# Softmax attention and a 2-D spectral filter in one kernel: the later weight pads on GpSimd, one small product on ScalarE, and a new planned order

## The chip, the cores and the metric

The kernel runs on one core of a Trainium2 chip. A core has five engines, each with its own instruction queue that runs in order: TensorE (PE, matmuls; PEld in the profile is its weight load), VectorE (DVE), ScalarE (ACT), GpSimd (POOL) and SyncE (SP, which here issues most of the DMAs). The metric is the device time of one execution in microseconds; lower is better. Times of the kernel before are those of three runs, and the profile is of one more execution.

## The reference

One input `x` of 2048 rows and 448 columns goes through two branches, which a gate mixes row by row:

```python
g = sigmoid((x * gate_w).sum(-1, keepdims=True))
a = softmax_attention(x, wqkv) @ wo        # 16 heads of 28 columns, no mask
b = irfft2(rfft2(x) * (w_r + 1j * w_i))    # over both axes, S=2048, D=448
return g * a + (1 - g) * b
```

Attention has 16 heads x 2048 x 2048 scores. All tensors are bfloat16.

## The kernel before

**Attention.** The heads are taken in four groups of four. A head's 28 columns are padded to 32, so that four heads fill the 128 partitions: `Wp` holds the padded query and key weights. Group 0's weights are padded early on POOL (`pq0`, `pk0`), those of groups 1 to 3 later on DVE (`pq1`, `pk1`, line 479), as copies from the raw weights (`raw`, which the profile shows as `Z`, whose space it uses) to `Wp`. They wait for the loads `wq1` and `wk1`, which a small POOL write each releases on SP. Queries are projected in chunks of 512 (`qT`), keys into `kT`, values into `V`.

The scores are made in tiles of 128 keys x 512 queries for one head: 1024 tiles, in 16 chunks of 64. A tile is exponentiated in one of two ways. ACT reads one or two neighbouring PSUM banks and writes `exp` into `PA` (line 1276; early tiles go into `oT`, whose space is free then). Or DVE writes an integer form of the exponent into `PD` (line 1300), and POOL adds two constants to groups of up to three such tiles (line 1108, two instructions a group); the three integer tiles, read as bfloat16, are each multiplied by `V`, and their sum approximates the exponential. So an ACT tile costs PE one score and one value matmul, and a DVE tile one score and three value matmuls. Value matmuls add up in a PSUM bank for a chunk, which is then normalised (`normalise`) and later multiplied by `Wo`.

Matmuls are narrow. A score uses 30 rows of TensorE's array, and four heads can run side by side ("row" mode); a value matmul uses 32 columns, and four can run side by side ("col" mode). `mc` splits a wide matmul into such strips.

**Squares and the largest key.** Keys and queries carry a column with half their squared length. For it a projected chunk is squared, either by ACT (`e_pj_sq`, line 696) or by DVE in two instructions (`e_pj_sd`, lines 702 and 704). The parameter `qdn` says how many of the 16 query chunks, counted from the last, use DVE: 15 here. For groups 1 to 3 a chain `largest` (`kw1` to `kw3`) finds the longest key: POOL squares the keys (`e_ks`, line 737), a matmul adds them up, DVE takes a maximum (`e_kx_m1`, line 745), DVE multiplies a 128 x 4 constant by it (`e_kx_sp`, line 748, tile `m1`), a matmul transposes that, DVE takes a maximum again (line 754), a matmul spreads it and DVE copies it (line 760). The queries of the group need the result.

**The filter.** POOL folds `x` (`e_xf`, lines 845 and 847: `xr` and in place `xt`, four passes of each), then come matmuls with constant tables in stages F1 to F6, with DVE evictions between (lines 856, 893, 906, 923, 936 to 938).

**Order.** Nothing is scheduled while it runs. A planner in the kernel's own Python places every task in time by simple costs per engine (ACT 0.051 us + columns/1200, DVE 0.065 us + columns/960) and a latency between engines, and the program is the list of tasks in that order; each engine then runs its own part in order, with semaphores. Units (a projection, a filter stage) have a target time, `target + OFF[name]`, and the dictionary `PAR` has the limits by which score tiles are shared out: `dve_lead` and `pool_lead` (how far DVE's and POOL's planned work may run ahead when DVE takes a tile), `n_dve` (the most tiles for DVE), `hold`, `slack` and `cp` (when DVE stops taking tiles of a chunk), `k3`, `w3`, `w2` (which run of banks ACT is given), `a21`. With `a21` over 0 a third score tile joins a pair as a single ACT tile only if ACT's planned backlog is at most `a21` microseconds; with 0 this test is left out:

```python
            if PAR["a21"] > 0 and P.backlog("ACT") > s + PAR["a21"]:
                return None
```

POOL tasks that are ready are taken by key, lowest first; `xr` and `xe` of block k have the keys 0.5 k and 0.5 k + 0.1 (about -5 for k = 0).

Of the kernel before, what the change touches and what calls it, by code (L numbers as in the profile page):

```python
# [12 lines left out]
ACT = mybir.ActivationFunctionType  # L13
ALU = mybir.AluOpType
# [151 lines left out]
def cols(n):  # L166

    return max(n / 2400.0 + 0.003 + 0.000016 * n, 0.026)


def dve(n):

    return 0.065 + n / 960.0


def act(n):
    return 0.051 + n / 1200.0
# [124 lines left out]

class Kernel:

    PAR = dict(T=368, margin=0, dve_lead=1.065, pool_lead=10.679, early=374.528, dmargin=0.3, join=0.1, veff=0.9, vnext=4, vnb=3, nfa=2, nfd=2, flush=0.2, hold=4, n_dve=380.349, late=8, fill=1, cp=1.617, slack=0.884, zgap=0.6, vurg=24.799, nfa2=5, nfd2=0, trk=0.361, vrk=2.7, fitm=0.02, ukeep=3, dkeep=0, k3=2, w3=0.3, w2=0.091, amax=2, ulate=16.42, dsolo=0, k21=0, a21=1, qdn=15)


    OFF = dict(X0=5.19, X1=-27.98, X3=0.84, X5=5.45, X6=-20.0, q0_0=-17.13, k0_0=0.4, k0_0b=14.3, k0_1=31.05, k0_2=-0.87, k0_3=24.59, v0_0=-34.41,
               v0_1=5.02, v0_2=34.02, v0_3=39.07, q0_1=-26.85, q0_2=-9.67, q0_3=-1.37, gate=-42.87, F1_0=21.01, F1_1=-0.1, F1_2=-18.79, F1_3=10.64,
               F1_4=6.41, F1_5=-3.3, F1_6=13.27, F1_7=-3.83, F1_8=-19.35, F1_9=-37.58, F1_10=-31.96, F1_11=-3.0, F1_12=8.24, F1_13=12.19, F1_14=10.6,  # L310
               F1_15=3.05, k1_0=-6.72, k1_1=11.73, k1_2=-10.54, k1_3=2.77, kw1=-2.6, v1_0=59.93, v1_1=-7.41, v1_2=33.97, v1_3=16.69, q1_1=3.56,
               q1_2=31.48, q1_3=43.95, F2_0=-56.04, F3_0=39.53, F5_0=34.29, F2_1=-37.91, F3_1=-1.85, F5_1=20.99, F2_2=-0.01, F3_2=13.06, F5_2=15.59,
               F2_3=-0.41, F3_3=24.43, F5_3=21.39, F2_4=-20.67, F3_4=-0.44, F5_4=-15.95, F2_5=-51.59, F3_5=20.45, F5_5=30.74, F2_6=-22.67,
               F3_6=-11.91, F5_6=0.76, F2_7=15.58, F3_7=-27.34, F5_7=40.78, F2_8=-45.05, F3_8=-2.08, F5_8=1.99, F2_9=1.89, F3_9=-4.53, F5_9=5.02,
               F2_10=-20.81, F3_10=-2.03, F5_10=-2.65, F2_11=-61.46, F3_11=-48.73, F5_11=6.72, F2_12=-31.48, F3_12=4.76, F5_12=-2.58, F2_13=8.64,
               F3_13=-22.22, F5_13=-47.39, F2_14=37.5, F3_14=29.27, F5_14=1.07, F2_15=-29.45, F3_15=10.64, F5_15=1.27, k2_0=-1.49, k2_1=-12.56,
               k2_2=-0.3, k2_3=-2.61, kw2=18.08, q2_0=17.63, v2_0=18.18, v2_1=0.51, v2_2=50.32, v2_3=17.26, q2_1=3.35, k3_0=4.85, k3_1=-26.48,
               k3_2=17.52, k3_3=-22.9, kw3=-30.88, q3_0=13.8, v3_0=-18.7, v3_1=-4.44, v3_2=21.94, v3_3=-1.69, q3_1=0.48, q2_2=-0.95, q3_2=1.88,
               q2_3=0.3, rg0=-13.79, rg1=-54.48, rg2=-36.06, rg3=-18.67, F6_0=-50.79, F6_1=5.4, F6_2=-3.55, F6_3=-15.05, F6_4=-36.03, F6_5=-0.33,
               F6_6=-35.14, F6_7=-32.01, F6_8=-28.36, F6_9=-21.44, F6_10=-29.11, F6_11=-16.4, F6_12=-3.59, F6_13=-18.37, F6_14=-0.2, F6_15=-2.28,  # L320
               o_0=25.95, o_1=8.69, o_2=-0.63, o_3=3.15, o_4=48.45, o_5=31.19, o_6=-15.24, o_7=27.38, o_8=18.41, o_9=5.1, o_10=-1.7, o_11=13.87,
               o_12=29.43, o_13=5.28, o_14=16.72, o_15=-1.66)


    NB = 8
# [96 lines left out]
    def head(self):  # L422
# [3 lines left out]
        dep = self.dep = {}  # L426
# [31 lines left out]
        gate = {}  # L458
# [16 lines left out]
        def pad(name, eng, qk, g0, g1, deps, dur, key=-8):  # L475
            src = self.raw[:, :, 448 * qk + 112 * g0:448 * qk + 112 * g1].rearrange("p c (h d) -> p c h d", d=28)
            o = self.Wp[0:112, :, qk, 4 * g0:4 * g1, 0:28]
            e = {"DVE": nc.vector, "POOL": nc.gpsimd}[eng]
            dep[name] = P.add(eng, dur, lambda: e.tensor_copy(out=o, in_=src), deps=deps + [m], key=key)
# [4 lines left out]
        for s in range(4):  # L484
            dep[f"wo{s}"] = P.add("SP", 0.42, lambda s=s: self.dma(self.Wo[32 * s:32 * s + 28, :, :], wo4[s]),
                                  deps=[dep["woz"]], land=8.0, key=50)
        pad("pq1", "DVE", 0, 1, 4, [dep["wq1"]], 0.75, -0.4)
        pad("pk1", "DVE", 1, 1, 4, [dep["wk1"]], 0.75, -0.4)

        for r, src in enumerate((self.w_r, self.w_i)):  # L490
            s3 = src.rearrange("(a b) f -> a b f", b=128)
# [19 lines left out]
    def make_units(self):  # L511
        U = self.U = {}
        dep = self.dep
        T = self.T = self.PAR["T"]

        def unit(name, target, phases, deps=(), **k):
            u = U[name] = Unit(name, target + self.OFF.get(name, 0.0), phases, deps, **k)
            self.P.units.append(u)
            return u
# [12 lines left out]
        def proj(qk, g, c, target):  # L532
# [14 lines left out]
            sq = [("ACT", act(512), self.e_pj_sq, (qk, g, c))]  # L547
            if qk == 0 and n >= 16 - self.PAR["qdn"]:
                sq = [("DVE", dve(512), self.e_pj_sd, (qk, g, c, 0)), ("DVE", dve(512), self.e_pj_sd, (qk, g, c, 1))]
# [37 lines left out]
        def largest(g, t0):  # L587

            unit(f"kw{g}", t0, [("PE", cols(512), self.e_kx_pe, (g,), "col"), ("DVE", 0.62, self.e_kx_m1, (g,)),
                                ("DVE", 0.1, self.e_kx_sp, (g,)), ("PE", 0.03, self.e_kx_tr, (g,), "col"), ("DVE", 0.25, self.e_kx_mm, (g,)),  # L590
                                ("PE", 0.04, self.e_kx_bc, (g,), "col"), ("DVE", 0.12, self.e_kx_kc, (g,))],
                 [dep[f"ks{g}_{c}"] for c in range(4)] + [dep["cA2"], dep["mxz"]], rank=-1)
        nc = self.nc
# [19 lines left out]
        for c in range(4):  # L613
            proj(1, 1, c, (0.10 + 0.025 * c) * T)
        largest(1, 0.18 * T)
        proj(0, 1, 0, 0.20 * T)
        values(1, 0.21 * T, 0.01 * T)
# [5 lines left out]
        for c in range(4):  # L623
            proj(1, 2, c, (0.30 + 0.03 * c) * T)
        largest(2, 0.40 * T)
        proj(0, 2, 0, 0.42 * T)
        values(2, 0.43 * T, 0.015 * T)
        proj(0, 2, 1, 0.5 * T)
        for c in range(4):
            proj(1, 3, c, (0.515 + 0.015 * c) * T)  # L630
        largest(3, 0.565 * T)
        proj(0, 3, 0, 0.575 * T)
        values(3, 0.58 * T, 0.01 * T)
# [111 lines left out]
        self.nc.vector.tensor_reduce(out=self.mc1[:], in_=b, axis=AX.X, op=ALU.max)  # L745

    def e_kx_sp(self, b, g):
        self.nc.vector.tensor_scalar(out=self.m1[:], in0=self.cA[:, 685:689], scalar1=self.mc1[:, 0:1], scalar2=None, op0=ALU.mult)  # L748

    def e_kx_tr(self, b, g):  # L750
        self.mm(b[0:4, 0:4], self.cA[:, 681:685], self.m1[:], pos=(0, 0))
# [253 lines left out]
    def stream(self):  # L1005
        P, nc, U, PAR = self.P, self.nc, self.U, self.PAR
        packs = [[(n, g, c, i, h) for i in range(16) for h in range(4)] for n, (g, c) in enumerate(self.chunks)]
# [65 lines left out]
        def take_dve(busy, k):  # L1073
            out = []
            for n in range(st["chunk"], 16):
                L = [p for p in packs[n] if p not in busy]
                if n == 15:
                    L = L[:max(0, len(L) - int(PAR["hold"]) - 4)]
                elif len(packs[n]) <= PAR["hold"]:
                    continue  # L1080
                elif max(P.backlog("POOL"), P.free["PE"]) + PAR["cp"] > P.free["PE"] + 0.36 * len(packs[n]) + PAR["slack"]:
                    continue
# [573 lines left out]
```

## Time and profile before

| | |
|---|---|
| time, median of 3 runs | 375.91 us (375.65 to 376.28) |
| the profiled execution | 376.95 us, its span 375.2 us |
| mean granted TensorE clock | 0.986 |
| PE busy | 363.3 us, 97% of the span |
| ACT busy | 355.2 us, 95% |
| DVE busy | 327.9 us, 87% |
| POOL busy | 319.6 us, 85% |

The profiled execution took 1.04 us more than the median of the runs. Lines of the profile read: engine or line, operation, output tile <- input tile with its shape, count, then busy microseconds, mean nanoseconds of one, idle time just before them and what ended it. In a timeline row the first number is the start and the second the time, both in microseconds, and what stands in brackets is the idle time of that engine ahead of it, with its releaser; neighbouring instructions of a kind are merged (x3). In a row of waits stand the waiting engine and line, what it waited for, and then the total, the number of times and the longest.

### The profile page before, as it was taken

How to read it: one execution, taken by the hardware profiler on the slowest of the kernel's cores; microseconds unless marked ns; L12 is line 12 of the kernel's file. 1: busy time of each engine (PE TensorE's matmuls, PEld its weight loads, DVE VectorE, ACT ScalarE, POOL GpSimd, SP SyncE). 2: the span in 40 equal slices, each digit the busy share in tenths (PEclk: the TensorE clock that was granted, in tenths of full speed). 3: DMA queues.
4: the chain of work that ended last, by engine and by line, in shares of the span. 5: the costliest groups of instructions: out<-in, count | busy, mean ns of one | idle time of the engine just before them, and what ended most of it. 6: DMA issues, size and time to landing. Idle time of an engine off the chain costs nothing.

```text
span 375.2 us, 15055 instructions
## 1 busy us (share of the span) xinstructions
PE 363.3 (97%) x6526; PEld 140.4 (37%) x6526; DVE 327.9 (87%) x564; ACT 355.2 (95%) x411; POOL 319.6 (85%) x262
## 2 busy tenths in 40 slices
PE   8979999999999999999999999999999999999995
PEld 5434332334334334344343433333333333233332
DVE  5696899989996999999999789899999899998962
ACT  3977999999999999999999999999999999999993
POOL 7953789997899989988799998869988899899991
PEclk9977999999999999999999999999999999999999
DMA  8654400000000012112111021100000000001001
GB/s 263 137 105 66 129 27 3 2 3 3 28 3 18 28 28 59 42 42 79 48 45 28 17 57 30 37 21 3 3 2 14 28 14 14 2 17 38 26 15 51
DMA packets 18968, 14.77 MB, mean 39 GB/s; under 512 B 7923, under 2 KB 18517, under 8 KB 18902
## 3 DMA queue, kind: packets, MB, share of 16 engines
q1 hardware_dynamic: 17542, 13.01, 13.0%
q8 instruction: 51, 0.84, 1.0%
q10 hardware_dynamic: 1360, 0.81, 0.8%
q14 instruction: 15, 0.12, 0.1%
HBM read 11.97 MB, written 3.68 MB: 42 GB/s over the span
## 4 chain that ended last, share of the span: by engine, by line
PE 59%; ACT 22%; DVE 12%; issue 4%; DMA 1%; POOL 1%; DVEq 0%; SPq 0%; ACTq 0%
PE bank L400 58%; ACT PA L1276 22%; DVE PD L1300 5%; PE bank L678 1%; DMA Z<-in_A_wqkv_dram 1%; DVE AB L936 1%; DVE xt L938 1%; DVE sq L704 1%; DVE xt L937 1%; DVE sq L702 1%; DVE m L748 1%; DVE kT L717 0%; DVE mc L745 0%; DVE oraw L969 0%; POOL xr L845 0%
## 5 line engine op out<-in xcount | busy, mean ns | idle before, releaser
L1276 ACT ACTIVATE PA<-bank 128x1024 bf16<-128x1024 f32 (+1 forms) x386 | 340.4, 1088 | 7.1 <-PE bank L400 6.6
L1108 POOL TENSOR_SCALAR PD<-PD 128x1536 int16<-128x1536 int16 (+2 forms) x190 | 269.0, 1417 | 40.5 <-DVE PD L1300 24.5
L1300 DVE TENSOR_SCALAR PD<-bank 128x512 int16<-128x512 f32 x273 | 180.1, 682 | 16.7 <-PE bank L400 14.6
L400 PE MATMUL bank<-qT,kT 30*128 30x512 bf16 x1024 | 143.8, 387 | 2.6 <-DVE kT L717 2.1
L400 PE MATMUL bank<-PD,V 128*32 128x512 bf16 x819 | 120.4, 383 | 0.0
L400 PE MATMUL bank<-PA,V 128*32 128x512 bf16 x735 | 118.1, 383 | 0.0
L400 PEld LDWEIGHTS <-kT 30*128 30x128 bf16 (+1 forms) x1040 | 38.4, 91 | 121.1 <-issue 114.2
L400 PEld LDWEIGHTS <-V 128*32 128x32 bf16 x1570 | 32.6, 94 | 43.3 <-issue 39.6
L400 PE MATMUL bank<-xT,Wp 112*32 112x512 bf16 (+3 forms) x528 | 40.8, 388 | 0.5 <-DVE PD L1300 0.2
L400 PE MATMUL bank<-Wv,xT 112*32 112x112 bf16 (+1 forms) x1024 | 19.9, 225 | 0.1
L400 PE MATMUL bank<-Wo,oT 128*32 128x448 bf16 x256 | 18.6, 356 | 0.3 <-DVE oT L988 0.3
L400 PEld LDWEIGHTS <-xT 112*32 112x32 bf16 x1024 | 15.3, 102 | 6.6 <-issue 6.1
L906 DVE TENSOR_TENSOR TT<-bank,Wf 128x900 bf16<-128x900 f32 x16 | 17.3, 1085 | 0.5 <-PE bank L400 0.5
L400 PEld LDWEIGHTS <-Wp 112*32 112x32 bf16 (+1 forms) x528 | 10.5, 96 | 15.4 <-issue 12.1
L737 POOL TENSOR_TENSOR oT<-kT 128x512 bf16<-128x512 bf16 x12 | 12.4, 1040 | 0.5
L923 DVE CAST Z<-bank 113x512 bf16<-113x512 f32 x16 | 10.8, 684 | 1.9 <-PE bank L400 1.7
L913 POOL TENSOR_TENSOR TT<-TT 128x225 bf16<-128x225 bf16 x16 | 9.0, 562 | 3.4 <-DVE TT L906 2.8
L988 DVE TENSOR_TENSOR oT<-bank,oraw 128x512 bf16<-128x512 f32 (+1 forms) x19 | 11.1, 599 | 0.7 <-PE bank L400 0.6
L717 DVE CAST kT<-bank 128x512 bf16<-128x512 f32 x15 | 10.1, 677 | 1.6 <-PE bank L400 1.6
L856 DVE CAST U__76<-bank 113x512 bf16<-113x512 f32 x16 | 10.6, 680 | 0.5 <-PE bank L400 0.5
L704 DVE TENSOR_TENSOR sq<-bank,sq 128x512 bf16<-128x512 f32 x15 | 10.4, 690 | 0.5
L702 DVE CAST sq<-bank 128x512 bf16<-128x512 f32 x15 | 10.2, 681 | 0.5 <-PE bank L400 0.5
(91 smaller groups left out, 283.9 us busy)
## 6 DMA issues: line engine op xcount, KB each, us to landing
cM<-cM SPq DMA_DIRECT2D x16, 128.0 KB, 2.2
cG<-cG SPq DMA_DIRECT2D x16, 128.0 KB, 2.1
Wf<-Wd SPq DMA_DIRECT2D x32, 56.2 KB, 2.3
out_dram<-fin SPq DMA_DIRECT2D x15, 112.0 KB, 1.7
xt<-in_A_x_dram SPq DMA_DIRECT2D x2, 448.0 KB
Z<-in_A_wqkv_dram SPq DMA_DIRECT2D x2, 294.0 KB
Wd<-in_B_w_r_dram SPq DMA_DIRECT2D x4, 112.5 KB, 6.2
Wd<-in_B_w_i_dram SPq DMA_DIRECT2D x4, 112.5 KB, 9.1
```

Source lines behind the costliest of these rows:

```text
L400: self.nc.tensor.matmul(out, lhsT=lhsT, rhs=rhs, start=start, stop=stop, skip_group_check=True, **k)
L702: self.nc.vector.tensor_copy(out=t, in_=b)
L704: self.nc.vector.tensor_tensor(out=t, in0=b, in1=t, op=ALU.mult)
L717: self.nc.vector.tensor_copy(out=self.kT[g % 2][:, 512 * c:512 * c + 512], in_=b)
L737: self.nc.gpsimd.tensor_tensor(out=self.oT[:, 3, 512 * c:512 * c + 512], in0=k, in1=k, op=ALU.mult)
L856: self.nc.vector.tensor_copy(out=o, in_=b[0:113, :].rearrange("p (c g e) -> p c g e", c=4, g=16))
L906: self.nc.vector.tensor_tensor(out=self.TT[bg % 2][:].rearrange("p w r f -> p w (r f)").rearrange("p w (r f) -> p w r f", r=2), in0=bc_at( ...
L923: self.nc.vector.tensor_copy(out=self.Z[:, :, :, :, 8 * bg:8 * bg + 8].rearrange("p c t s e -> p c (t s) e"), in_=b[0:113, :].rearrange("p ...
L988: nc.vector.tensor_tensor(out=self.oT[:, g, 512 * c + c0:512 * c + c1], in0=b[:, c0:c1], in1=oraw[:, c0:c1], op=ALU.mult)
L1108: nc.gpsimd.tensor_scalar(out=t[:, j, 0:n, :], in0=t[:, 0, 0:n, :], scalar1=float(sh), scalar2=1.0, op0=ALU.add, op1=ALU.mult)
L1276: nc.scalar.activation(out=buf, in_=src, func=ACT.Exp, scale=LN2 / 128.0)
L1300: nc.vector.tensor_scalar(out=dst, in0=self.bank[b], scalar1=C2, scalar2=0.0, op0=ALU.add, op1=ALU.max)
```

## The change

Three edits are in the code, and the planner's numbers are replaced. The pads of the later query and key weights go from DVE to POOL, with a planned 1.4 us instead of 0.75 and a key of -2 instead of -0.4. The small product in `largest` goes from DVE to ACT, with a planned 0.2 us instead of 0.1. All of `PAR` but `T` and a few others, and all of `OFF`, have new values; they were chosen outside the kernel, by an objective with a penalty on plans that use little of TensorE's array. That objective is not part of the code.

```diff
-    PAR = dict(T=368, margin=0, dve_lead=1.065, pool_lead=10.679, early=374.528, dmargin=0.3, join=0.1, veff=0.9, vnext=4, vnb=3, nfa=2, nfd=2, flush=0.2, hold=4, n_dve=380.349, late=8, fill=1, cp=1.617, slack=0.884, zgap=0.6, vurg=24.799, nfa2=5, nfd2=0, trk=0.361, vrk=2.7, fitm=0.02, ukeep=3, dkeep=0, k3=2, w3=0.3, w2=0.091, amax=2, ulate=16.42, dsolo=0, k21=0, a21=1, qdn=15)
+    PAR = dict(T=368, margin=0, dve_lead=1.156, pool_lead=14, early=807.331, dmargin=0.3, join=0.6, veff=0.95, vnext=2.765, vnb=2, nfa=6.029, nfd=2.924, flush=0.8, hold=2, n_dve=290, late=8, fill=1, cp=2.032, slack=2, zgap=0.25, vurg=25, nfa2=5, nfd2=0, trk=0.441, vrk=2.574, fitm=0.019, ukeep=3, dkeep=0, k3=3, w3=0, w2=0.2, amax=2, ulate=12, dsolo=0, k21=0, a21=0, qdn=8)
-    OFF = dict(X0=5.19, X1=-27.98, X3=0.84, X5=5.45, X6=-20.0, q0_0=-17.13, k0_0=0.4, k0_0b=14.3, k0_1=31.05, k0_2=-0.87, k0_3=24.59, v0_0=-34.41,
+    OFF = dict(X0=-0.45, X1=-29.9, X2=-10.5, X3=-11.1, X4=-4.99, X5=-7.62, X6=-28.51, X7=-25.13, k0_0=-4.85, k0_0b=10.57, k0_1=22.47, k0_2=-20.78,
...
-        pad("pq1", "DVE", 0, 1, 4, [dep["wq1"]], 0.75, -0.4)
-        pad("pk1", "DVE", 1, 1, 4, [dep["wk1"]], 0.75, -0.4)
+        pad("pq1", "POOL", 0, 1, 4, [dep["wq1"]], 1.4, -2)
+        pad("pk1", "POOL", 1, 1, 4, [dep["wk1"]], 1.4, -2)
...
-                                ("DVE", 0.1, self.e_kx_sp, (g,)), ("PE", 0.03, self.e_kx_tr, (g,), "col"), ("DVE", 0.25, self.e_kx_mm, (g,)),
+                                ("ACT", 0.2, self.e_kx_sp, (g,)), ("PE", 0.03, self.e_kx_tr, (g,), "col"), ("DVE", 0.25, self.e_kx_mm, (g,)),
...
     def e_kx_sp(self, b, g):
-        self.nc.vector.tensor_scalar(out=self.m1[:], in0=self.cA[:, 685:689], scalar1=self.mc1[:, 0:1], scalar2=None, op0=ALU.mult)
+        self.nc.scalar.activation(out=self.m1[:], in_=self.cA[:, 685:689], func=ACT.Copy, scale=self.mc1[:, 0:1])
```

More of the change, by code (lines that the diff above doesn't have):

```diff
@@ L303 @@
 class Kernel:
-    PAR = dict(T=368, margin=0, dve_lead=1.065, pool_lead=10.679, early=374.528, dmargin=0.3, join=0.1, veff=0.9, vnext=4, vnb=3, nfa=2, nfd=2, flush=0.2, hold=4, n_dve=380.349, late=8, fill=1, cp=1.617, slack=0.884, zgap=0.6, vurg=24.799, nfa2=5, nfd2=0, trk=0.361, vrk=2.7, fitm=0.02, ukeep=3, dkeep=0, k3=2, w3=0.3, w2=0.091, amax=2, ulate=16.42, dsolo=0, k21=0, a21=1, qdn=15)
-    OFF = dict(X0=5.19, X1=-27.98, X3=0.84, X5=5.45, X6=-20.0, q0_0=-17.13, k0_0=0.4, k0_0b=14.3, k0_1=31.05, k0_2=-0.87, k0_3=24.59, v0_0=-34.41,
[L309 to L322, printed above, removed]
@@ new lines @@
+    PAR = dict(T=368, margin=0, dve_lead=1.156, pool_lead=14, early=807.331, dmargin=0.3, join=0.6, veff=0.95, vnext=2.765, vnb=2, nfa=6.029, nfd=2.924, flush=0.8, hold=2, n_dve=290, late=8, fill=1, cp=2.032, slack=2, zgap=0.25, vurg=25, nfa2=5, nfd2=0, trk=0.441, vrk=2.574, fitm=0.019, ukeep=3, dkeep=0, k3=3, w3=0, w2=0.2, amax=2, ulate=12, dsolo=0, k21=0, a21=0, qdn=8)
+    OFF = dict(X0=-0.45, X1=-29.9, X2=-10.5, X3=-11.1, X4=-4.99, X5=-7.62, X6=-28.51, X7=-25.13, k0_0=-4.85, k0_0b=10.57, k0_1=22.47, k0_2=-20.78,
+               k0_3=32.55, kw0=10.25, v0_0=-12.45, v0_1=-29.57, v0_2=6.17, v0_3=32.53, q0_1=4.21, q0_2=-6.73, gate=15.58, F1_0=36.12, F1_1=0.69,
+               F1_2=-1.75, F1_3=17.53, F1_4=-13.39, F1_5=13.41, F1_6=16.94, F1_7=9.72, F1_8=0.25, F1_9=-25.08, F1_10=-51.88, F1_11=0.2, F1_12=5.78,
+               F1_13=26.43, F1_14=-2.48, F1_15=-2.49, k1_0=-8.16, k1_1=17.54, k1_2=2.77, k1_3=8.36, kw1=13.88, q1_0=-1.45, v1_0=52.1, v1_1=-1.06,
+               v1_2=39.22, v1_3=12.53, q1_1=10.96, q1_2=34.23, q1_3=45.93, F2_0=-52.96, F3_0=34.06, F5_0=-3.69, F2_1=-40.46, F5_1=18.45, F2_2=-4.76,
+               F3_2=-5.56, F5_2=38.59, F2_3=-5.36, F3_3=12.45, F5_3=0.43, F2_4=5.71, F3_4=-3.25, F5_4=-14.08, F2_5=13.74, F3_5=16.41, F5_5=-11.6,
+               F2_6=-1.94, F3_6=7.43, F5_6=-13.26, F2_7=13.57, F3_7=-6.19, F2_8=-55.51, F3_8=37.14, F5_8=-21.59, F2_9=-45.03, F3_9=-20.95,
+               F2_10=-1.55, F3_10=-32.87, F5_10=-26.13, F2_11=-48.8, F3_11=-43.35, F5_11=9.26, F2_12=-38.78, F3_12=1.02, F5_12=-0.32, F2_13=23.39,
+               F3_13=7.44, F5_13=-20.63, F2_14=14.62, F3_14=53.26, F5_14=-2.45, F2_15=-3.06, F3_15=16.65, F5_15=0.78, k2_0=-13.88, k2_1=6.57,
+               k2_2=-10.56, k2_3=-95.43, kw2=15.14, q2_0=33.8, v2_0=3.08, v2_1=-1.03, v2_2=28.31, v2_3=-2.27, q2_1=20.53, k3_0=-3.14, k3_1=-38.98,
+               k3_2=-15.49, k3_3=-42.81, kw3=1.34, q3_0=7.3, v3_0=-17.34, v3_1=-5.49, v3_2=42.42, v3_3=12.22, q3_1=-16.25, q3_2=-13.01, q2_3=-0.81,
+               q3_3=17.97, rg0=-5.85, rg1=-56.51, rg2=-35.51, rg3=-19.61, F6_0=-32.88, F6_1=-4.28, F6_2=0.57, F6_3=-2.16, F6_4=-1.15, F6_5=-49.81,
+               F6_7=-2.74, F6_8=25.8, F6_9=-11.59, F6_10=-16.07, F6_11=-39.7, F6_12=18.45, F6_13=-30.87, F6_14=17.71, F6_15=-0.8, o_0=38.37,
+               o_1=10.8, o_2=8.04, o_3=34.48, o_4=51.74, o_5=6.44, o_6=25.61, o_7=-2.77, o_8=-27.63, o_9=-2.51, o_10=-2.02, o_11=7.52, o_14=8.79,
+               o_15=-10.28)
```

## The prediction

> **What bounds the kernel now.** I read the page's engine shares first, then the busy time by stretch, then the waits of the two poor stretches, then the order of instructions where those waits end.
>
> ```profile
> PE 363.3 (97%) x6526; PEld 140.4 (37%) x6526; DVE 327.9 (87%) x564; ACT 355.2 (95%) x411; POOL 319.6 (85%) x262
> L1276 ACT ACTIVATE PA<-bank 128x1024 bf16<-128x1024 f32 (+1 forms) x386 | 340.4, 1088 | 7.1 <-PE bank L400 6.6
> 10.50:19.00 8.50, 7.97 (x125) 3.66 (x125) 5.01 (x7) 8.46 (x13) 8.34 (x5) 1.00 0.53 122
> 19.00:24.00 5.00, 2.43 (x32) 1.22 (x31) 4.93 (x9) 3.07 (x5) 3.93 (x3) 0.94 0.59 119
> 24.00:34.00 10.00, 10.00 (x231) 5.31 (x232) 6.66 (x15) 6.96 (x10) 3.81 (x4) 0.52 0.59 95
> 46.00:365.00 319.00, 315.54 (x5666) 117.19 (x5664) 293.16 (x504) 317.14 (x360) 285.30 (x224) 1.00 0.09 25
> 370.00:375.20 5.20, 1.07 (x20) 0.41 (x16) 2.04 (x6) 1.16 (x2) 0.00 (x0) 0.98 0.27 91
> ```
>
> The stretch rows give PE, weight load, DVE, ACT and POOL busy, then PE's clock, DMA share and GB/s. From 46 to 365 us ACT is busy 317.14 of 319.00 us: the exponentials run back to back, and PE (315.54) is no looser. So time can only come from what ACT has to do, from the 7.1 us that it idles before exponentials, or from the end (5.2 us, which the edit doesn't address). Those idle times lie almost all before 34 us: 19 to 24 us has PE busy 2.43 of 5.00, and 24 to 34 us has PE "busy" all the time, but at a clock of 0.52.
>
> ```profile
> 16.13 1.88 POOL L847 TENSOR_TENSOR xt<-xt 128x896 bf16<-128x896 bf16 x1
> 16.88 3.60 DVE L479 COPY Wp<-Z 112x1344 bf16<-112x1344 bf16 x2 [0.41 <-DMA Z<-in_A_wqkv_dram]
> 17.96 2.14 POOL L845 TENSOR_TENSOR xr<-xt 128x896 bf16<-128x896 bf16 x1
> 18.12 0.40 PE L400 MATMUL bank<-sq,cA 128*32 128x512 bf16 x4
> 20.40 1.27 DVE L717 CAST kT<-bank 128x512 bf16<-128x512 f32 x2
> 21.13 0.39 PE L400 MATMUL bank<-qT,kT 30*128 30x512 bf16 x3 [2.07 <-DVE kT L717]
> 21.56 1.02 ACT L1276 ACTIVATE PA<-bank 128x1024 bf16<-128x1024 f32 x1 [1.87 <-PE bank L400]
> PE bank L400 <- DVE kT L717: 2.1, 1, 2.1
> ACT PA L1276 <- PE bank L400: 3.0, 5, 1.0
> ```
>
> One chain: the two late pads (L479) hold DVE from 16.88 to 20.40, the key casts behind them wait in DVE's order, PE idles 2.07 us for them, ACT 1.87. The last two rows are of waits: from 10.5 to 23.6 us PE has no longer one than this 2.1 us; and from 23.6 to 34.1 us, in the half-clock stretch ACT loses 3.0 us more.
>
> **The change, part by part.**
>
> *The late pads on POOL.* DVE loses its 3.60 us of pads, so the last key cast can follow its matmuls, which end at 18.52 in the rows above, and the 1.87 us wait of ACT goes. The loads of these weights on SP and the small POOL writes that release them stay as they are. What is late next is ACT itself: before that wait it was busy 8.46 of 8.50. On POOL the nearest row is its own smaller pad:
>
> ```profile
> L479 POOL COPY Wp<-Z 112x448 bf16<-112x448 bf16 x2 | 1.1, 556 | 1.7 <-DMA Z<-in_A_wqkv_dram 1.7
> POOL PD L1108 <- DVE PD L1300: 7.0, 2, 3.6
> ```
>
> Three times the elements is 3 x 0.556 = 1.7 us each, 3.3 us in all (at least 1.1, at most the 3.6 that DVE took). Their key (-2) puts them ahead of the remaining xr/xt passes, behind the same weight transfer, so these passes and the first-stage FFT matmuls that read them move back by some 3.3 us plus the wait for the transfer. I cost this at nothing: POOL waited 7.0 us between 23.6 and 34.1 us (the row above, from that stretch's waits). If that cover is gone, the price is those 3.3 us in the filling of PE, not on ACT.
>
> *The clock.* If PE isn't starved at 19 to 24 us, I expect the half-clock stretch to go and with it the 3.0 us of waits; bounds 0 and 3.0, and I take 3.0, since the drop follows directly on the only starved stretch of the run, and later stretches stand at 1.00. [...]
>
> *The largest key's small product on ACT.* L748 is now a DVE instruction:
>
> ```profile
> 134.29 3.02 POOL L1108 TENSOR_SCALAR PD<-PD 128x1536 int16<-128x1536 int16 x2
> 136.25 1.08 DVE L748 TENSOR_SCALAR m<-cA,mc 128x4 bf16<-128x4 bf16 x1
> 137.38 0.17 PE L400 MATMUL bank<-m,cA 128*4 128x4 bf16 x1 [0.76 <-DVE m L748]
> 138.14 1.09 ACT L1276 ACTIVATE PA<-bank 128x512 bf16<-128x512 f32 x2 [0.61 <-PE bank L400]
> 224.63 4.44 POOL L1108 TENSOR_SCALAR PD<-PD 128x1536 int16<-128x1536 int16 x3
> 226.58 0.98 DVE L748 TENSOR_SCALAR m<-cA,mc 128x4 bf16<-128x4 bf16 x1
> 228.65 1.02 ACT L1276 ACTIVATE PA<-bank 128x1024 bf16<-128x1024 f32 x1 [0.60 <-PE bank L400]
> L825 ACT ACTIVATE ge<-ge 128x16 f32<-128x16 f32 x1 | 0.3, 273 | 0.0
> ```
>
> Twice it takes about 1 us for four elements and ends with a POOL instruction (137.33 against 137.31; 227.56 against some 227.6); PE waits in order for it, then ACT loses 0.61 and 0.60. On ACT nothing ties it to POOL: gain 1.2. It costs ACT 3 x 0.27 = 0.8 by its nearest small instruction (L825); bounds 0 and, if ACT also stands waiting for the maximum, 3 x 0.9 = 2.7. Queued behind it are exponentials. [...]
>
> *qdn 15 to 8.* Seven query squares go from two DVE instructions (L702, L704) to one on ACT (L696):
>
> ```profile
> L702 DVE CAST sq<-bank 128x512 bf16<-128x512 f32 x15 | 10.2, 681 | 0.5 <-PE bank L400 0.5
> L704 DVE TENSOR_TENSOR sq<-bank,sq 128x512 bf16<-128x512 f32 x15 | 10.4, 690 | 0.5
> L696 ACT ACTIVATE sq<-bank 128x512 bf16<-128x512 f32 x4 | 2.5, 616 | 0.5 <-PE bank L400 0.5
> L1276 ACT ACTIVATE PA<-bank 128x1024 bf16<-128x1024 f32 x349 | 328.2, 1129 | 6.3 <-PE bank L400 5.7 <-ACT PA L1276 0.3
> L1300 DVE TENSOR_SCALAR PD<-bank 128x512 int16<-128x512 f32 x273 | 180.1, 682 | 16.7 <-PE bank L400 14.6 <-issue 0.4 <-ACT PA L1276 0.2
> L1108 POOL TENSOR_SCALAR PD<-PD 128x1536 int16<-128x1536 int16 x170 | 249.9, 1470 | 27.4 <-DVE PD L1300 12.4 <-PE bank L400 2.8 <-DVE mx L754 0.8
> L400 PE MATMUL bank<-PD,V 128*32 128x512 bf16 x819 | 120.4, 383 | 0.0
> ```
>
> ACT overlaps the tails: two 512-wide ones took 1.09 us at 138.14, one alone 0.62 (616 ns), so one more costs 1.09 - 0.62 = 0.48. Seven: +3.4 on ACT, which has nothing to hide them. DVE gets back 7 x 1.37 = 9.6.
>
> *More score tiles on DVE.* DVE is freed of 3.6 + 9.6 + 2.4 (three L748, mean 0.79) = 15.6 us. A tile takes 180.1 / 273 = 0.66 there, so 23 more at most; the cap n_dve = 290 allows 17. POOL pays 2 x 1.47 / 3 = 0.98 for each; 17 would take 16.7 of the 33.7 us that POOL idles from 46 to 365, with pads outside that. Lower bound 0. I take the middle, 9. ACT is relieved by half a pair each, 328.2 / 349 / 2 = 0.47: -4.2. PE pays two extra value matmuls per tile, at most 2 x 0.38 / 4 = 0.19 each when four share a pass: 1.7, out of the 2.07 + 0.76 + some 5 (ten microseconds at half clock) that it gets back.
>
> *a21 = 0.* A third, single score tile may now join a pair at any backlog. Two singles instead of a pair cost 2 x 0.48 - 0.94 = 0.02. Between 0 and 100 more singles that is 0 to 1; I take 0.5.
>
> *The order.* The new offsets move nearly every unit. A tile of work moved isn't work added, and with ACT and PE full I take 0; the trace of before gives no row for it, so I bound it by the 3.5 us that PE idles from 46 to 365 us, to either side.
>
> **Sum on ACT's line:** -1.9 - 3.0 - 1.2 + 0.8 + 3.4 - 4.2 + 0.5 = -5.6 us. The profiled execution, span 375.2, took 376.95, which is 1.04 above the median of the runs; 376.95 - 5.6 = 371.4, and against the median 375.91 - 5.6 = **370.3 us**.
>
> **The rivals.**
> *The half clock stays.* The early order remains thin on PE whatever DVE does (loads, transposes and casts are still dependent on each other), so the 3.0 us stay: 375.91 - 2.6 = 373.3. For it: the drop came after a stretch with PE at 2.43 of 5.00, not after an empty one. Against: the pads are the named releaser of the largest gap in that stretch. [...]
>
> *No difference.* The pads on POOL wait for the transfer in POOL's order, xr/xt come late, PE lacks filler, and the early ACT waits move rather than go. Then -4.9 becomes 0 and what is left is -0.7: 375.2, inside 0.2% (0.75 us, about what this measurement can tell from no change). For it: the passes queued behind the pads. Against: 7.0 us of POOL idle next to them.
>
> *Slower: ACT's added work isn't bought back.* If DVE takes no more tiles than now, the sum is -1.4. If new bank use (a third tile takes a bank) lets it take fewer, each adds 0.47: from 270 tiles on nothing is gained, and at 263, ten fewer, it is -1.4 + 4.7 = +3.3: 379.2. For it: DVE's tiles already wait for PE for 14.6 us, and ACT has no slack. Against: the freed 15.6 us.
>
> **How the numbers follow.** Full forecast 0.47, its own range 367 to 373; half clock stays 0.19; no difference 0.11; slower 0.23. Faster by over 0.2% is 0.47 + 0.19 = 0.66, within it 0.11, slower 0.23. The lower end takes all 17 tiles (another -3.8: 366.5); the upper end takes in half of the slow case and stops at 378.
>
> **What would show it.** L479 on POOL at about 1.7 us; key casts at 18.6 to 19.5 us with no 2 us gap on PE; a clock of 1.00 from 19 to 34 us and ACT above 9 of each 10 us there; seven more L696; L748 on ACT, and no 0.6 us gaps of ACT near the largest keys; L1300 at about 282. The forecast is wrong if the clock row shows 0.5 anywhere after 10 us, or if L1300's count falls below 270.

## The result, and the profile after

The changed kernel took 371.52 us, the median of four runs (370.52 to 372.58), against 375.89 before: a ratio of 0.988 (95% interval 0.985 to 0.992). The profiled execution has a span of 370.8 us against 375.2.

The lines of the page of after, and its busy time by stretch (same columns as before):

```profile
PE 362.0 (98%) x6552; PEld 139.9 (38%) x6552; DVE 317.9 (86%) x550; ACT 355.2 (96%) x414; POOL 325.6 (88%) x262
L1276 ACT ACTIVATE PA<-bank 128x1024 bf16<-128x1024 f32 (+1 forms) x381 | 338.9, 1107 | 1.5 <-PE bank L400 1.4
L1300 DVE TENSOR_SCALAR PD<-bank 128x512 int16<-128x512 f32 x278 | 184.5, 684 | 22.4 <-PE bank L400 19.7
19.00:24.00 5.00, 4.76 (x85) 2.14 (x78) 4.27 (x10) 5.00 (x7) 3.82 (x4) 1.00 0.58 109
24.00:34.00 10.00, 8.07 (x266) 4.36 (x254) 5.71 (x14) 8.59 (x14) 8.08 (x6) 1.00 0.58 100
46.00:365.00 319.00, 318.07 (x5715) 118.38 (x5707) 286.33 (x492) 317.73 (x364) 288.11 (x224) 1.00 0.09 24
```

ACT is busy for 355.2 us in both kernels, to the tenth. What went is its idle time: 7.1 us before exponentials are now 1.5. From 19 to 24 us PE is busy 4.76 of 5.00 us (2.43 before), and from 24 to 34 us the clock stands at 1.00, where it stood at 0.52.

The early order of instructions in after:

```profile
17.00 0.68 DVE L717 CAST kT<-bank 128x512 bf16<-128x512 f32 x1
17.09 2.55 POOL L479 COPY Wp<-Z 112x1344 bf16<-112x1344 bf16 x2 [0.77 <-DMA Z<-in_A_wqkv_dram]
18.51 0.69 DVE L717 CAST kT<-bank 128x512 bf16<-128x512 f32 x1 [0.23 <-PE bank L400]
20.50 0.68 DVE L717 CAST kT<-bank 128x512 bf16<-128x512 f32 x1
23.76 1.89 POOL L847 TENSOR_TENSOR xt<-xt 128x896 bf16<-128x896 bf16 x1
30.43 0.36 PE L400 MATMUL bank<-Wv,xT 112*32 112x113 bf16 x13 [1.65 <-issue]
31.18 1.94 ACT L1276 ACTIVATE PA<-bank 128x1024 bf16<-128x1024 f32 x2 [1.41 <-PE bank L400]
```

The pads run on POOL, each key cast follows its matmuls, and POOL's remaining folding passes come at 23.76 us and later. The last two rows are new: in the middle of a run of value matmuls PE stops for 1.65 us with no engine as releaser, and this is nearly all that ACT still loses.

The small products, by group:

```profile
L748 ACT ACTIVATE m<-cA,mc 128x4 bf16<-128x4 bf16 x3 | 1.3, 435 | 0.0
```

From 36 us on, ACT no longer waits for PE before any exponential, where it had lost 0.61 and 0.60 us behind L748.

### The profile page after: what moved, and what is told of

It reads as the page before. It is cut to its first block, busy times and chain, and to the rows that moved or that the text cites. A ratio compares the mean times of both kernels' runs of the same rounds, so it can differ in the third digit from the quotient of the medians.

```text
span 370.8 us, 15120 instructions
## 1 busy us (share of the span) xinstructions
PE 362.0 (98%) x6552; PEld 139.9 (38%) x6552; DVE 317.9 (86%) x550; ACT 355.2 (96%) x414; POOL 325.6 (88%) x262
## 4 chain that ended last, share of the span: by engine, by line
PE 66%; ACT 26%; issue 3%; DVE 2%; DMA 2%; ACTq 0%; DVEq 0%
PE bank L400 65%; ACT PA L1276 24%; DMA xt<-in_A_x_dram 2%; PE bank L678 1%; ACT oT L1276 1%; DVE PD L1300 1%; ACT sq L696 0%; ACTq L410 0%; DVE xt L938 0%; DVE AB L936 0%; DVE xt L937 0%; DVE oT L988 0%; DVEq L1651 0%; DVE qT L715 0%; DVE sq L704 0%
## 5 line engine op out<-in xcount | busy, mean ns | idle before, releaser
L1276 ACT ACTIVATE PA<-bank 128x1024 bf16<-128x1024 f32 (+1 forms) x381 | 338.9, 1107 | 1.5 <-PE bank L400 1.4
L1108 POOL TENSOR_SCALAR PD<-PD 128x1536 int16<-128x1536 int16 (+1 forms) x188 | 273.0, 1452 | 31.4 <-DVE PD L1300 13.5
L1300 DVE TENSOR_SCALAR PD<-bank 128x512 int16<-128x512 f32 x278 | 184.5, 684 | 22.4 <-PE bank L400 19.7
L400 PE MATMUL bank<-PD,V 128*32 128x512 bf16 x834 | 121.7, 383 | 0.0
L400 PE MATMUL bank<-PA,V 128*32 128x512 bf16 x730 | 121.0, 383 | 0.0
L400 PE MATMUL bank<-xT,Wp 112*32 112x512 bf16 (+3 forms) x528 | 39.6, 377 | 0.2
L717 DVE CAST kT<-bank 128x512 bf16<-128x512 f32 x15 | 10.3, 685 | 2.3 <-PE bank L400 2.3
L893 DVE CAST AB<-bank 128x448 bf16<-128x448 f32 x16 | 9.9, 620 | 1.7 <-PE bank L400 1.6
L400 PE MATMUL bank<-cG,TT 128*32 128x256 bf16 (+1 forms) x256 | 10.8, 274 | 0.0
L969 DVE CAST oraw<-bank 128x512 bf16<-128x512 f32 x15 | 10.2, 681 | 0.1
```

The lines of the kernel that those rows point to most:

```text
L400: self.nc.tensor.matmul(out, lhsT=lhsT, rhs=rhs, start=start, stop=stop, skip_group_check=True, **k)
L717: self.nc.vector.tensor_copy(out=self.kT[g % 2][:, 512 * c:512 * c + 512], in_=b)
L893: self.nc.vector.tensor_copy(out=self.AB[bg % 2][:, 0:448], in_=b[:, 0:448])
L969: o1 = [P.add("DVE", dve(512), lambda: nc.vector.tensor_copy(out=oraw[:], in_=pv), deps=[last] + prev, key=-3, then=freed)]
L1108: nc.gpsimd.tensor_scalar(out=t[:, j, 0:n, :], in0=t[:, 0, 0:n, :], scalar1=float(sh), scalar2=1.0, op0=ALU.add, op1=ALU.mult)
L1276: nc.scalar.activation(out=buf, in_=src, func=ACT.Exp, scale=LN2 / 128.0)
```

## The experiments

Apart from the last one, every kernel here keeps the planned order of before ("b_") or of after ("a_") and changes only what its edit shows (a_wd_late moves transfers alone). Lines that an edit adds move the line numbers: L481 or L482 in an experiment is L479 of the two kernels, L726 is L717, L854 is L845, L1110 is L1108, and L1280 or L1281 is L1276. Medians of before, run beside them, are 375.7 to 376.0 us.

**b_pads_pool: the pads alone.**

```diff
 e = {"DVE": nc.vector, "POOL": nc.gpsimd}[eng]
+if name in ("pq1", "pk1"):
+    e = nc.gpsimd
```

> The order of before, every instruction in its place; only the two later weight pads are issued on POOL instead of DVE. Theory 1 (the pads on DVE starve PE, and the half clock follows from that): key casts at 18 to 19.5 us, clock 1.00 throughout, ACT's early waits of 1.9 + 3.0 us gone: 375.9 - 4.9 = 371.0 us. Theory 2 (the gain of the change is in its new order, the pads alone do little): a clock of 0.5 somewhere between 20 and 36 us is still there, and the time is 374.5 us or more.

372.65 us (371.49 to 377.01, twelve runs), ratio 0.992 (0.989 to 0.995). Its busy time by stretch:

```profile
19.00:24.00 5.00, 4.16 (x75) 1.97 (x71) 4.93 (x11) 4.95 (x8) 4.92 (x4) 1.00 0.57 120
24.00:34.00 10.00, 10.00 (x319) 5.30 (x317) 8.68 (x19) 10.00 (x15) 8.65 (x8) 1.00 0.51 96
```

ACT is full from 24 to 34 us: the early waits of 4.9 us are gone, with none of the new numbers. So theory 1 holds for the waits. But the median is 1.65 us above the 371.0 expected, and the runs spread widely. The mean clock of each says why in part: eight runs with a clock of at least 0.995 have a median of 372.3, four with 0.986 to 0.991 one of 375.5. The half clock comes back in some runs, though the pads are on POOL in all of them.

**b_warm and b_fill: zeros on PE.** Both add nine matmuls of zeros ahead of one score of before; b_warm's edit hit a score at 30 us, b_fill's the one that waits.

```diff
+        self.ns += 1
+        if self.ns == 17:
+            for _ in range(9):
+                self.mm(out, self.zz[:, 0:128], self.zz)
         r = slice(32 * h, 32 * h + 30)
```

> The order of before, with nine 128x512 matmuls of zeros added on PE ahead of the first score that waits for the third key cast, into a bank that this score overwrites. The pads stay on DVE, so the wait itself stays. Theory 1 (the half clock follows from PE standing empty for 2 us): clock 1.00 throughout, ACT's wait of 1.9 us stays, the 3.0 us after it go: 375.9 - 3.0 = 372.9 us. Rival (the half clock comes from thin use of the array in general, not from this gap): clock still 0.5 for about 10 us and 375.9 us, or more by the added matmuls.

377.69 us (ratio 1.004, 1.002 to 1.006): the zeros ran at 30.2 us, behind the half clock (22.2 to 29.0 us in this profile), and took 2.1 us of PE. They missed the gap, so this tests neither theory.

> The order of before, pads on DVE; nine 128x512 matmuls of zeros are added on PE right ahead of its 17th score, the one that stood waiting from 19.07 to 21.13 us, into the bank that this score then overwrites (in the earlier try the zeros came at 30 us, not in the gap). Theory 1 (the half clock follows from PE standing empty in that gap): clock 1.00 from 19 to 34 us, ACT's wait of 1.9 us stays and the 3.0 us behind it go: 375.9 - 3.0 = 372.9 us. Rival (the wait alone costs the time, the half clock is hidden or has another cause): 375.5 us or more.

374.30 us (ratio 0.996, 0.994 to 0.998). Its stretches, and its waits from 10.5 to 36 us:

```profile
19.00:24.00 5.00, 4.95 (x52) 2.02 (x41) 4.85 (x8) 3.17 (x6) 3.83 (x3) 1.00 0.58 121
24.00:34.00 10.00, 9.37 (x319) 5.46 (x320) 9.05 (x19) 10.00 (x15) 4.50 (x5) 1.00 0.52 93
ACT PA L1281 <- PE bank L401: 1.8, 1, 1.8
```

This separates the two parts. The wait stays (1.8 us), since the pads are still on DVE, but PE isn't empty, the clock stays at 1.00, and ACT's 3.0 us of waits behind it are gone: the span is 372.2, 3.0 below before's. The median gained half of the 3.0 expected, 1.5 us. Two of the twelve runs were still below 0.995, but that doesn't explain it, since the other ten have a median of 374.2, which is 1.5 below before's 375.8 as well. The 3.0 came from one execution of before that was longer than most (see the table below).

**a_pads_dve and a_pads_dve_busy: the pads back on DVE, in the new order.**

```diff
+if name in ("pq1", "pk1"):
+    e = nc.vector
```

> The order of after, every instruction in its place; only the two later weight pads are issued on DVE again. Theory 1: the key casts and evictions behind the pads come 3 us late, PE is empty for about 2 us, the half clock is back: 371.5 + 1.9 to 4.9 = 373.4 to 376.4 us. Theory 2 (the new order keeps PE fed whatever the pads do): clock 1.00 and 371.5 to 372.3 us.

371.62 us (370.69 to 372.83), ratio 0.988 (0.985 to 0.991): the same as after. Theory 1 fails for the new order. The pads by source line, first in before, then here (minimum, median, maximum in ns):

```profile
L479 DVE COPY Wp<-Z x2: 1496/1840/2185, 16.9 to 18.3; 112x1344 bf16<-112x1344 bf16 x2
```

```profile
L481 DVE COPY Wp<-Z x2: 502/502/502, 17.5 to 18.5; 112x1344 bf16<-112x1344 bf16 x2
19.99 3.00 POOL L1110 TENSOR_SCALAR PD<-PD 128x1536 int16<-128x1536 int16 x2 [3.55 <-PE bank L400]
```

The same copy on the same engine takes 0.50 us, not 1.5 and 2.2, and the second row shows what differs: POOL stood idle for 3.55 us until 19.99. In before it ran its folding passes beside the pads: the passes at 16.13 and 17.96 us ended at 18.01 and 20.11, and the two pads at 18.37 and 20.48, each some 0.4 us later.

In a_pads_dve_busy POOL copies the same raw weights beside the pads:

```diff
+nc.gpsimd.tensor_copy(out=self.U_[0:112, 0:4, 0:336], in_=self.raw[:, :, 448 * qk + 112:448 * qk + 448])
 e.tensor_copy(out=o, in_=src)
```

> The order of after, pads issued on DVE, and beside each of them POOL copies as many elements of the same raw weights to a place that is still unused. With POOL idle the two pads took 0.50 us each in this order. If a DVE copy from SBUF to SBUF stands still while a POOL instruction runs: the pads take 1 to 2 us each, the key casts come 1.5 to 2.5 us late, ACT loses 0.5 to 2 us: 372 to 373.5 us. If the two don't touch: 0.50 us each and 371.5 us.

371.71 us (370.81 to 372.35): the pads took 0.50 and 1.01 us, the first less than expected, since POOL's first copy was over (17.66 us) when it came, and the time didn't move. The second pad ended at 19.69 us, again some 0.4 us after POOL's copy beside it (19.33). It works the other way too: that POOL copy had started just after the first pad (17.73 and 17.66 us) and took 1.60 us, the other one 1.30. In this order a key cast stands between the two pads, not behind both.

**b_pool_wait: POOL held back instead, in the old order.**

```diff
 e.tensor_copy(out=o, in_=src)
+# once, behind the second pad:
+nc.gpsimd.memset(self.raw[0:1, 0, 112:113], 0.0)
+nc.gpsimd.memset(self.raw[0:1, 0, 560:561], 0.0)
```

> The order of before, both pads on DVE. One thing is added: two one-element writes on POOL, on cells that the pads have read, so that POOL's pass of line 845 that ran beside the second pad (17.96 to 20.10 us) starts only when both pads are done. If the pads' 3.6 us is made by the POOL passes beside them: the first pad still ends after the pass that runs when it starts (some 1.5 us), the second takes 0.50 us instead of 2.2, the casts come 1.7 us earlier, PE's gap shrinks from 2.07 to some 0.5 us, no half clock: 375.9 - 1.5 - 3.0 = 371.4 us. If DVE simply takes that long for these copies: the second pad again takes over 1.5 us, the half clock is back and the time 375.9 us or more.

372.62 us (372.02 to 375.30), ratio 0.992 (0.990 to 0.995), with both pads on DVE:

```profile
L482 DVE COPY Wp<-Z x2: 497/883/1269, 17.0 to 18.1; 112x1344 bf16<-112x1344 bf16 x2
18.75 1.88 POOL L854 TENSOR_TENSOR xr<-xt 128x896 bf16<-128x896 bf16 x1
18.77 1.29 DVE L726 CAST kT<-bank 128x512 bf16<-128x512 f32 x2
19.00:24.00 5.00, 4.16 (x71) 1.96 (x67) 4.86 (x11) 4.95 (x8) 4.30 (x3) 0.90 0.60 131
```

The second pad takes 0.497 us once nothing runs on POOL, and the casts start at 18.77, not 20.40. So what made the pads dear was the POOL pass beside them. The clock in the last row is a surprise: the 2 us gap on PE is gone (its weight load waits 0.19 us for the cast, and no wait of PE is over 0.5 us), and yet this profiled run dropped to half clock; of the seven runs two have a mean clock of 0.989.

**b_sp_act, b_both and a_sp_dve: the small product.**

```diff
-self.nc.vector.tensor_scalar(out=self.m1[:], in0=self.cA[:, 685:689], scalar1=self.mc1[:, 0:1], scalar2=None, op0=ALU.mult)
+self.nc.scalar.activation(out=self.m1[:], in_=self.cA[:, 685:689], func=ACT.Copy, scale=self.mc1[:, 0:1])
```

> The order of before, with the three small products on ACT and the pads left on DVE. If the 0.76 and 0.72 us for which PE waited for them were set by POOL's instruction beside them: L748 takes some 0.4 us on ACT, these two waits and ACT's 0.6 us behind each go, 375.9 - 0.6 = 375.3 us. Rival: ACT now stands waiting for DVE's maximum with exponentials queued behind it, and the time is 375.9 to 377 us.

375.11 us, ratio 0.998 (0.996 to 0.9995): the time is as expected, and the gain small. From 36 to 366 us ACT waits 0.6 us in all (three times, the longest 0.2) instead of 1.6. PE's own waits did not go as expected: it stands waiting for the product on ACT for 1.3 us (three times, the longest 0.6), where it waited 1.5 us for the one on DVE.

> The order of before, every instruction in its place, with both code edits: the pads issued on POOL and the three small products on ACT. None of the new planner numbers. By ACT's account, before idles 7.2 us between its first and last exponential; the pads take away 5.1 of it and the products 1.2, for 3 x 0.19 us more work: 375.9 - 5.7 = 370.2 us. If the new planner numbers brought something of their own, this stays above after: 372 us or more.

372.50 us (371.55 to 375.32), ratio 0.991 (0.988 to 0.995); the profiled span, 369.8, is below after's. By spans the old order with both edits is as good as after. By the medians of runs it is 1.0 us slower, with ranges that overlap: four of six had a clock below 0.995, with a median of 373.2, and two at 0.995 or more, at 371.7.

> The order of after, with the three small products back on DVE. If a POOL instruction beside them holds them up, as in before: about 1 us where one runs, PE waits 0.7 us and ACT 0.6 us behind each such place: 371.5 + 0.6 to 1.8 - 0.6 (ACT no longer does them) = 371.5 to 372.7 us, with 0.6 us waits of ACT between 36 and 366 us. If nothing runs on POOL there: 0.3 us each, no wait, 371 us.

371.89 us (371.71 to 373.67), ratio 0.991 (0.989 to 0.993): the median is within after's range. L748 took 0.75, 0.37 and 0.56 us, and PE's waits for it were 0.20 and 0.34 us, so the new order again is less sensitive to the place. No run puts both the pads and the products back in this order.

**a_sq_dve: the seven squares back on DVE.**

```diff
+if qk == 0 and (g, c) != (0, 0):
+    self.e_pj_sd(b, qk, g, c, 0)
+    self.e_pj_sd(b, qk, g, c, 1)
+    return
 self.nc.scalar.activation(out=self.sq[(c + qk) % 2][:], in_=b, func=ACT.Square)
```

> The order of after, but the seven query squares that qdn = 8 gives to ACT are done by two DVE instructions each at the same places. ACT's work falls by 7 x 0.48 = 3.3 us and DVE's grows by 7 x 1.3 = 9.1 us. If ACT's work alone sets the time: 371.5 - 3.3 = 368.2 us. If DVE, in this order, has no room just there, its evictions come late, PE and then ACT wait up to 0.9 us at each of the seven places: 371 to 374 us, with new waits of ACT for PE between 36 and 320 us.

376.24 us, ratio 1.000 (0.998 to 1.003): the whole gain is gone, more than was expected at worst. Its stretches, and its waits from 36 to 366 us:

```profile
19.00:24.00 5.00, 4.38 (x59) 1.78 (x55) 4.72 (x10) 4.62 (x6) 3.86 (x3) 0.90 0.62 124
24.00:34.00 10.00, 10.00 (x257) 5.35 (x256) 6.30 (x15) 7.31 (x11) 6.64 (x5) 0.71 0.50 87
ACT PA L1280 <- PE bank L400: 3.2, 8, 1.0
```

The half clock is back in nine of twelve runs, and later ACT waits eight times. The half clock isn't all of it: the one run with a clock of 0.998 still took 374.29 us. ACT's busy total fell by 1.2 us (to 354.0), not by 3.3, and that is worth less than the order that the squares were planned for.

**a_wd_late: the filter weights' transfers later.**

```diff
+wd = [t for k, t in self.dep.items() if isinstance(k, str) and k.startswith("wd")]
+order = [t for t in self.P.order if t not in wd]
+at = max(order.index(self.dep[f"wo{s}"]) for s in range(4)) + 1
+self.P.order = order[:at] + [t for t in self.P.order if t in wd] + order[at:]
```

> The order of after, with the 24 transfers that rearrange the filter weights in DRAM moved on SP behind the four loads of the output weights, so that they start after 30 us instead of at 9 to 36 us. After has a gap of 1.65 us on PE at 28.8 us that no engine released, and ACT waits 1.41 us behind it. Theory A (PE ran out of instructions, since the transfer that brings the next ones came late behind these transfers): the gap goes and the time is 371.5 - 1.4 = 370.1 us. Rival B (the gap has another cause): the gap stays, 371.5 us.

371.64 us (371.03 to 372.31), the same as after. PE's gap without a releaser is still there, 0.8 us by the waits, with the DMAs' share at 0.22 instead of 0.58 from 24 to 34 us. It was 1.0 us in a_pads_dve, without any change to the transfers. In after a 16 KB transfer of instructions had started at 27.99 us, 0.6 us ahead of the gap in the weight loads (28.61 to 30.43 us). That fits PE running out of instructions, but it isn't shown: before has such a transfer at 29.91 us, and PE is busy 10.00 us from 24 to 34 us.

**r_newnum_oldcode: the new numbers with the old code.** The planner makes its own order here.

> The new planner numbers with the code of before: the planner is told that the pads and the small products are on DVE (0.75 and 0.1 us), and makes an order of its own from the new PAR and OFF. If the numbers carry the gain by themselves: 371.5 to 372.5 us, clock 1.00. If the gain is in where the pads and products run: the half clock and 0.6 us waits are back, 374 to 377 us.

389.29 us, ratio 1.036 (1.034 to 1.039). Its exponentials of one tile, against 32 such in after:

```profile
L1276 ACT ACTIVATE PA<-bank 128x512 bf16<-128x512 f32 x89 | 55.2, 666 | 0.0
L1300 DVE TENSOR_SCALAR PD<-bank 128x512 int16<-128x512 f32 x267 | 175.0, 682 | 24.7 <-PE bank L400 22.2 <-POOL PD L1108 0.2 <-POOL TT L913 0.2
```

More tiles go through ACT, and more of them alone: its busy total is 364.6 us, 9.4 more than in before and after, and all four runs have a clock of at most 0.991. The numbers aren't good in themselves: they belong to one order, and with the pads and products elsewhere the planner arrives at another one, which is far worse.

**What the runs say together.** Each run's mean clock tells about how long the half clock lasted. It is set beside PE's busy time from 19 to 24 us of the one profiled execution of each kernel:

| kernels | PE busy, 19 to 24 us | runs with a clock under 0.995 | runs at 0.995 |
|---|---|---|---|
| before, beside the experiments | 2.43 of 5 | 74 of 75 | 1 |
| b_sp_act | 2.63 | 11 of 11 | 0 |
| b_pads_pool, b_both, b_pool_wait | 4.16 | 10 of 25 | 3 |
| a_sq_dve | 4.38 | 9 of 12 | 2 |
| after, a_pads_dve, a_pads_dve_busy, a_wd_late, a_sp_dve | 4.57 to 4.76 | 0 of 25 | 2 |
| b_fill (zeros) | 4.95 | 2 of 12 | 2 |

The profiled execution of before was a long one. Its half clock lasted 10.24 us, with a mean clock of 0.986; in b_sp_act, b_pool_wait and a_sq_dve it lasted some 6.8 us, with 0.988 to 0.991 (an estimate from their stretch rows: in a_sq_dve 0.90 over 5 us and 0.71 over 10 us make 3.4 us lost at a clock of 0.5). Of the 75 runs of before, 22 have a clock of 0.986 or less and a median of 376.5 us, and 52 have 0.988 to 0.991 and one of 375.7.

The column at 0.995 needs care. A half clock as long as the difference of those two lengths, 3.4 us, would give about that mean (an estimate: 0.5 x 3.4 / 372 is 0.0046), and the clock's fall behind the last matmuls, 2.2 us in before and 1.7 us in after by their clock records, would give 0.997 if the span held all of the 2.2. The two runs in the fifth row are the slowest of their kernels (372.83 and 373.67 us). No trace of them was kept, so it isn't known whether their clock dipped early.

Nor is the busy share a rule. With zeros it is highest, and two runs still fell. And after has a stretch as thin, around PE's stop, in which the clock stays at 1.00:

```profile
28.00:29.00 1.00, 0.78 (x51) 0.61 (x51) 1.00 (x3) 1.00 (x2) 1.00 (x1) 1.00 0.66 107
29.00:30.00 1.00, 0.00 (x0) 0.00 (x0) 0.19 (x1) 0.77 (x2) 1.00 (x2) 1.00 0.76 124
30.00:31.00 1.00, 0.57 (x16) 0.29 (x15) 0.00 (x0) 0.00 (x0) 0.24 (x1) 1.00 0.69 127
```

That is 1.35 of 3.00 us, a share of 0.45, against 0.49 in before from 19 to 24 us. So filling the early gap makes the half clock rarer in the old order (b_fill, 2 of 12 runs against 74 of 75), but what exactly brings it on stays open.

## Why the prediction was right

The time forecast was 370.3 us, and 371.5 was measured. The chain that it named (pads on DVE, late key casts, empty PE, half clock) is shown in the old order: b_pads_pool and b_pool_wait take away the slow pads, b_fill the empty PE, and the waits behind them go (in b_pool_wait's profile only the first, since its clock still fell). In after the same waits are gone, but a_pads_dve shows that there the new order would have removed them alone. So the early gain has two causes, each enough in the profiled executions, and the prediction named one.

By its steps, on ACT's line of the two profiled executions:

- *Early waits, -1.9 and -3.0.* Measured: both gone, and b_fill parts them as forecast (1.8 stays, 3.0 goes). By medians the 3.0 is too much: b_fill gained 1.5. The term was read from an execution with 10.24 us of half clock, where most runs of before have a clock like that of executions with some 6.8. A new gap of 1.41 us, behind PE's stop, had no step in the sum.
- *The small product, -1.2 and +0.8.* Measured: the two waits are gone; the three cost ACT 1.3 us of busy time, partly beside other work. In the old order (b_sp_act) the time gained 0.7 us.
- *Squares +3.4, tiles -4.2, singles +0.5.* Seven more L696 came, as said. The tiles were mis-sized: five more on DVE, not nine. Singles fell from 43 to 34 where more were expected. By its own prices that makes +1.8 with the product (0.8 + 3.4 - 5 x 0.47), yet ACT's busy total is 355.2 before and after. So some of these prices were too dear, and it is partly luck that the net of its terms (+0.5 with the product) came out so near.
- *The start.* Not in the sum: the first exponential began at 11.73 us instead of 10.52, +1.2. It lay between 11.05 and 11.78 in the other profiled runs of this order, and between 10.68 and 11.40 in those of the old one, so part of it is chance.

So -7.1 + 1.5 for the idle time and +1.2 for the start give the 4.4 us of the span.

Some signs that it named came otherwise. The pads took 1.31 us each on POOL, not 1.7; the third key cast came at 20.50 us, later than 19.5; ACT was busy 8.59 of 10 us from 24 to 34, because of PE's stop; L1300 reached 278, not 282. And ACT's idle times did not lie almost all before 34 us: of the 6.6 us that it waited for PE, 1.6 lay behind 36 us.

"The order" was set at 0. In time that is nearly so: b_both, with the old order, has a median 1.0 us above after's and a span 1.0 below. But the new order does something that a sum for one execution can't show: it makes the pads' place indifferent, and no run of the five kernels that keep it and its squares fell below 0.995. It is no safe place, since seven squares back on DVE bring the half clock back in nine of twelve runs. Of the rivals, "the half clock stays" was right in that the pads on POOL alone leave it to chance (4 of 12 runs). "No difference" put its cover in doubt for the folding passes; they moved behind 23 us and cost nothing that shows.

How long PE must starve before the half clock comes isn't shown by these runs. Zeros in a gap of 2.07 us took the half clock from 74 of 75 runs to 2 of 12, which is for the prediction's reading of the gap, but b_pool_wait fell to half clock with no wait of PE over 0.5 us.

## What to carry to other kernels

When a cheap copy on VectorE takes three times its time in the trace (here 1.50 us against 0.50), look at what GpSimd runs at that moment, and move either of the two. Where TensorE starves for 2 us, price the half clock behind it too: here it cost ACT 3.0 us in the profiled execution, beside 1.9 for the gap, and 1.5 us by the medians of b_fill. And look at the clock of every run, not of the profiled one alone: an order that avoids the half clock in one execution may meet it in the next (b_pads_pool did in 4 of 12 runs), and the profiled execution may be a dear one.

## What the runs showed of the hardware that was not expected

The same 112x1344 copy on VectorE took 0.50 us with GpSimd idle and up to 2.19 us beside its passes, and ended some 0.4 us after them. That a short instruction on VectorE can take several times as long beside one on GpSimd was suspected for the four-element product (1.08 and 0.98 us in before), and shown on the pads. The half clock depends on the run: in the kernels with PE busy 4.16 of 5 us in their profiles it came in 10 of 25 runs, and a stretch of after with 1.35 of 3 us went without it.
